# A GpSimd drain placed between the scatters of the last two experts

## The chip, the cores and the metric

The kernel runs on one core of one Trainium2 chip. The metric is the device time of one execution, in microseconds (us), start to end, with the closing barrier of the program inside it. The engines go by the profile's names: PE (TensorE matmul), PEld (TensorE weight load), DVE (VectorE), ACT (ScalarE), POOL (GpSimd) and SP (SyncE). A "q" behind an engine's name (POOLq, SPq) marks instructions of its queue that the profile does not count as busy: waits, branches, drains.

## The reference

The reference is a delta-rule attention followed by a mixture of experts. The attention (4 batches, 8 heads, 768 steps, head size 48) gives 3072 rows of 384 values. Each row goes to one of 8 experts:

```
logits = x @ w_gate;  expert_idx = argmax(logits)          # x: 3072 x 384
disp[e, counts[e]] = x[i]                                   # rows gathered by expert
h = relu(einsum('ecd,edf->ecf', disp, w1))                  # 384 -> 1024
y = einsum('ecf,efd->ecd', h, w2)                           # 1024 -> 384
out[i] = gate_w[i] * y[expert_idx[i], pos[i]]               # scattered back by token
```

## The kernel before

The first half of the program does the attention and, beside it, the routing: which expert each row goes to, and two tables of row numbers, one for gathering (`src_row`) and one for scattering (`dst_row`). The attention's rows are stored in a buffer in HBM (`xbuf`). The second half, from about 280 us on, is the loop `run` over the 8 experts, ordered by load (`NS`: 512 rows for the first down to 364 for the last).

For each expert the loop does five things. GpSimd issues indirect DMAs that fetch the next expert's weights (`fetch`, `weights`, five DMAs per expert, tile `rw`) and gather its rows (`gather`, tile `xg`). ACT and DVE split fetched weights into a high and a low part (`split`, tiles `hw` and `lw`). `first` computes the hidden layer, eight blocks of 128 columns with nine matmuls each (L1171); ACT takes the relu as the high part `hh` (L1173) and DVE the rest as `hl` (L1174). `second` or, for the experts whose row count fills its tiles well, `rows` computes the second product (L1191 or L1235). `scatter` then multiplies 128 rows by their gate on ACT (L1214, tile `ys`) and issues an indirect DMA on GpSimd that writes them to their places in the output (L1215).

The last two experts (`e` = 6 and 7) both go through `rows`, each in three blocks of rows: 128, 128 and 120 or 108. So each issues three scatters, right after one another in GpSimd's queue. Expert 6 prefetches for expert 7; expert 7 has no successor (`nx` is false), so nothing is fetched, gathered or split in it, and GpSimd has only the three scatters left.

GpSimd's queue runs in program order. Before each scatter stands a wait on the landing of the scatter ahead of it, and the scatter itself waits for ACT's `ys`. Behind the last scatter stand a load of the flag `more` with a branch (L1360, L1361: a general path that is not taken here), and then the program's end (L1421), which the framework writes: SP waits for every DMA that is still open, every engine has a drain, and all five engines meet in a barrier that GpSimd closes; GpSimd then clears the semaphores, and a second barrier follows. Over the program GpSimd issues 98 indirect DMAs: 40 for weights, 29 scatters and 29 gathers (25 of `xg` by `src_row`, and 4 of the first expert's rows).

The order in the second half is set by the framework's scheduler; `issue_after(x)` makes the instructions in its block come behind instruction `x` in the schedule. It adds no semaphore.

Of the kernel before, what the change touches and what calls it, by code (L numbers as in the profile page):

```python
# [54 lines left out]
class Attention:  # L55
# [448 lines left out]
    def run(self):  # L504
        with self.tc.manual_schedule(engines={mybir.EngineType.PE, mybir.EngineType.Activation, mybir.EngineType.DVE, mybir.EngineType.Pool, mybir.EngineType.SP}):
            self.run_()

    def run_(self):
# [16 lines left out]
        for i, (q, k0) in enumerate([(0, 0), (1, 0), (2, 0), (3, 0), (4, 0), (5, 0), (0, 1)]):  # L525
            run(self.scores(q, k0, 1 if i < 2 else 2, banks[i % 4]))
            if i < 2:
                self.causal.clear()
            elif i < 6:
                self.heat(8, HEATS[(i + 1) % 4])  # L530
            if i == 1:
                while not self.rooted:
                    spent += self.advance()
            for job in late[i]:
                job()

            while len(self.causal) > 2:
                while spent < EVICT[i - 2] and "Tc" not in self.sg[0]:
                    spent += self.advance()
                self.causal.pop(0)()  # L540
# [6 lines left out]
        for c in range(KC):  # L547
# [28 lines left out]
            if c == 0:  # L576
                self.update(c, 1, self.residual(c, 1))
                self.solves(c, 1)
                self.product_q(c)
                run(self.scores(1, 1))  # L580
# [427 lines left out]
class Experts:  # L1008
# [201 lines left out]
    def scatter(self, e, i, n, yp, ys=None):  # L1210
        nc, rt = self.nc, self.rt
        if ys is None:
            ys = self.pt.tile([128, DM], F32, name="ys", bufs=4)
        nc.scalar.activation(ys[:n], yp[:n], AF.Copy, scale=rt.gt[:n, i, e : e + 1])  # L1214
        nc.gpsimd.indirect_dma_start(  # L1215
            out=self.out[:, :],
            out_offset=bass.IndirectOffsetOnAxis(ap=rt.dst_row[:n, i, e : e + 1], axis=0),
            in_=ys[:n], in_offset=None, bounds_check=N - 1, oob_is_err=False,
        )
# [18 lines left out]
    def run(self):  # L1238
        for _ in self.split0:
            pass  # L1240
        x = self.x
        yT = None
        for e in range(E):
            nx = e + 1 < E
            if nx:
                for _ in self.fetch(e + 1) if e else self.loading:
                    pass
                xg = self.gather(e + 1)
            split = self.split(e + 1) if nx else iter(())
            hs = self.first(e, x, split, 0, 2)  # L1250
            if yT:
                self.last(e - 1, yT, split)
            hs += self.first(e, x, split, 2, 8)
            if nx:
                x = self.split_x(xg, e + 1)
            yT = None
            if e in DIRECT:
                self.rows(e, hs)
            else:
                yT = self.second(e, hs)  # L1260
            for _ in split:
                pass
# [162 lines left out]
```

## Time and profile before

| what | value |
|---|---|
| median of 3 runs | 519.18 us (518.07 to 519.61) |
| profiled execution | 516.17 us |
| its span, first to last instruction | 514.4 us |
| granted TensorE clock, mean | 0.929 of full speed |
| PE busy | 434.4 us (84%) |
| PEld busy | 382.6 us (74%) |
| DVE busy | 302.9 us (59%) |
| ACT busy | 232.9 us (45%) |
| POOL busy | 142.1 us (28%) |

The profiled execution lasted 516.17 us, of which 514.4 us lie between the first and the last instruction; 1.8 us lie around that span. Busy time counts work on an engine's datapath only. Waits, branches and drains are not in it, nor in the chain of waits, whose last entry is the last counted instruction. They are seen when one asks for a source line: the program's end is L1421 and its beginning L1415.

### The profile page before, as it was taken

The page shows a single profiled execution, that of the slowest core. Times are in us where ns is not written, and L with a number is a line of the kernel's source. Part 1 is how long each engine was busy: PE and PEld are TensorE (multiplying, and loading weights), DVE is VectorE, ACT ScalarE, POOL GpSimd, SP SyncE. Part 2 cuts the span into 40 slices and gives each one's busy share as a digit, 9 for nine tenths or more (in the row PEclk, how much of TensorE's full clock was granted, in tenths as well). Part 3 has the DMA queues.
Part 4 walks back from the last instruction along what each step waited for, and adds up shares of the span by engine and source line. Part 5 has one row for each costly group of instructions (what it writes and reads, how often), then busy time and mean ns, then how long its engine had stood idle before and what let it go on. Part 6 is the DMA issues. An engine that isn't in the chain of part 4 may idle for free. (4 is left out here: it accounts for less than half of the span.)

```text
span 514.4 us, 16636 instructions
## 1 busy us (share of the span) xinstructions
PE 434.4 (84%) x7010; PEld 382.6 (74%) x7020; DVE 302.9 (59%) x973; ACT 232.9 (45%) x549; POOL 142.1 (28%) x146
## 2 busy tenths in 40 slices
PE   5673558798997989688879989999999999999990
PEld 3343446676776777566769878899999999999990
DVE  2899899688989983435652565273350817263210
ACT  2115123455766666356522554273562828363210
POOL 8002000100000111456354273434143453520110
PEclk9995577878999999979988999999999999999996
DMA  8882477867866455753162174526145453620000
GB/s 212 189 249 80 114 195 206 246 188 195 208 196 162 99 139 134 197 174 105 34 203 105 55 281 156 169 87 198 72 159 170 152 189 98 204 78 17 29 32 14
DMA packets 51683, 74.45 MB, mean 145 GB/s; under 512 B 28571, under 2 KB 37717, under 8 KB 51602
## 3 DMA queue, kind: packets, MB, share of 16 engines
q1 hardware_dynamic: 39810, 31.78, 23.9%
q0 software_dynamic: 9280, 34.98, 20.0%
q10 hardware_dynamic: 2512, 6.55, 4.5%
q8 instruction: 57, 0.93, 0.8%
q14 instruction: 24, 0.20, 0.1%
HBM read 60.97 MB, written 12.43 MB: 143 GB/s over the span
## 5 line engine op out<-in xcount | busy, mean ns | idle before, releaser
L1174 DVE SCALAR_TENSOR_TENSOR hl<-hp,hh 128x256 fp32r<-128x256 f32 (+7 forms) x64 | 35.5, 555 | 100.2 <-ACT hh L1173 98.9
L1171 PE MATMUL hp<-xh,hw 128*128 128x444 f32 (+6 forms) x168 | 59.1, 354 | 0.0
L1171 PE MATMUL hp<-xl,hw 128*128 128x444 f32 (+6 forms) x168 | 58.1, 346 | 0.0
L1171 PE MATMUL hp<-xh,lw 128*128 128x444 f32 (+6 forms) x168 | 58.1, 346 | 0.0
L415 ACT COPY x<-s 48x384 f32<-48x384 f32 x92 | 43.6, 474 | 30.6 <-PE s L409 20.7
L1133 DVE TENSOR_TENSOR lw<-rw,hw 128x384 fp32r<-128x384 f32 (+1 forms) x100 | 56.4, 609 | 1.8 <-ACT hw L1132 1.8
L1215 POOL DMA_INDIRECT out_dram<-ys,dst_row x27 | 28.6, 1060 | 102.0 <-ACT ys L1214 60.7
L1132 ACT CAST hw<-rw 128x384 fp32r<-128x384 f32 (+1 forms) x103 | 51.6, 556 | 1.6 <-DMA out_dram<-pk,dst_row 1.6
L1273 POOL DMA_INDIRECT rw<-in_w_dram,widx x40 | 40.9, 1021 | 31.3 <-DVE lw L1133 17.7
L1173 ACT ACTIVATE hh<-hp 128x256 fp32r<-128x256 f32 (+7 forms) x64 | 31.4, 491 | 38.2 <-PE hp L1171 35.7
L388 PE MATMUL u<-R,T 64*64 64x48 f32 x736 | 32.5, 228 | 11.2 <-DVE R L378 10.9
L393 ACT ACTIVATE u<-u,mask 128x192 f32<-128x192 f32 x96 | 35.3, 419 | 14.6 <-PE u L388 14.0
L290 DVE TENSOR_TENSOR M<-M,tmp 128x30 f32<-128x30 f32 (+18 forms) x120 | 40.9, 341 | 0.1
L388 PEld LDWEIGHTS u<-R,T 64*64 64x64 f32 x736 | 27.8, 142 | 14.7 <-DVE R L378 13.8
L287 DVE TENSOR_TENSOR tmp<-M,AT 128x96 f32<-128x96 f32 (+33 forms) x124 | 38.5, 342 | 0.1
L378 DVE TENSOR_TENSOR R<-vs,ks 128x192 f32<-128x192 f32 x46 | 16.3, 353 | 31.8 <-PE ks L368 28.2
L1191 PE MATMUL yT<-hh,hw 128*128 128x444 f32 (+3 forms) x96 | 34.1, 359 | 0.0
L1191 PE MATMUL yT<-hh,lw 128*128 128x444 f32 (+3 forms) x96 | 33.8, 355 | 0.0
L1191 PE MATMUL yT<-hl,hw 128*128 128x444 f32 (+3 forms) x96 | 33.0, 354 | 0.0
L1171 PEld LDWEIGHTS hp<-xh,hw 128*128 128x128 f32 x168 | 31.6, 188 | 0.7
L177 PE MATMUL gw<-kb,kd 112*32 112x128 f32 x384 | 18.3, 348 | 16.3 <-DVE P L155 6.7
L1171 PEld LDWEIGHTS hp<-xl,hw 128*128 128x128 f32 x168 | 31.6, 188 | 0.4
(226 smaller groups left out, 982.2 us busy)
## 6 DMA issues: line engine op xcount, KB each, us to landing
kb<-in_kqf_dram SPq DMA_DIRECT2D x24, 192.0 KB
xbuf<-xt SPq DMA_DIRECT2D x24, 192.0 KB
kq<-in_kqf_dram ACTq DMA_DIRECT2D x10, 448.0 KB
kq<-in_kqf_dram SPq DMA_DIRECT2D x10, 448.0 KB
v<-in_vt_dram SPq DMA_DIRECT2D x22, 192.0 KB
k<-in_kt_dram SPq DMA_DIRECT2D x21, 192.0 KB
kd<-in_kqf_dram SPq DMA_DIRECT2D x12, 224.0 KB
mb<-M SPq DMA_DIRECT2D x5, 512.0 KB
```

Of the source, the lines that this page charges most:

```text
L287: nc.vector.tensor_tensor(tv, col.unsqueeze(3).to_broadcast([128, k, m, n]), row.unsqueeze(2).to_broadcast([128, k, m, n]), ALU.mult)
L290: return lambda: nc.vector.tensor_tensor(out, out, tv, alu)
L388: nc.tensor.matmul(us[rows[p], m], T[rows[p], 4 * g + m].rearrange("p a b -> p (a b)"), R[rows[p], m], start=True, stop=True,)
L393: nc.scalar.activation(U[:, 4 * g : 4 * g + 4, o], us, AF.Copy, scale=self.mask[:, 32 + o : 33 + o])
L415: nc.scalar.copy(Xn[rows, ts, :, a].rearrange("p t (h r) d -> p t h r d", h=2), self.S[rows, :, ts].rearrange("p h t r d -> p t h r d"),)
L1132: (nc.scalar.copy if e else self.hi)(hi[p], raw[p])
L1133: (nc.vector.tensor_tensor if e else self.lo)(lo[p], raw[p], hi[p], ALU.subtract)
L1171: nc.tensor.matmul(hp, a, b, start=i == 0, stop=i == len(terms) - 1)
L1173: act = nc.scalar.activation(hh, hp, AF.Relu)
L1174: after = nc.vector.scalar_tensor_tensor(hl, hp, 0.0, hh, ALU.max, ALU.subtract)
L1191: self.nc.tensor.matmul(yT[m], a, b, start=j == 0, stop=j == len(terms) - 1)
L1273: nc.gpsimd.indirect_dma_start(out=raw[:, i * st : i * st + st].rearrange("p k m -> p (k m)"), out_offset=None, in_=tab[:, :], in_offset=b ...
```

## The change

The change keeps a handle on the last scatter that was issued, and in the last expert, behind `first`, it puts one drain instruction on GpSimd that is ordered behind that scatter. At that point of the loop the last scatter is the third one of expert 6.

```diff
@@ scatter
-        nc.gpsimd.indirect_dma_start(
+        self.sent = nc.gpsimd.indirect_dma_start(
             out=self.out[:, :],
...
@@ run
             hs += self.first(e, x, split, 2, 8)
+            if not nx:
+                with self.tc.issue_after(self.sent.ins):
+                    self.nc.gpsimd.drain()
             if nx:
                 x = self.split_x(xg, e + 1)
```

All other instructions of all five engines keep their place, their waits and their addresses; lines behind the loop are numbered 3 higher. GpSimd's queue around the drain is this (drains are left out of such a listing; `ys` numbers tell the scatters apart, the first three are expert 6's, the last three expert 7's):

```order
L1215 DMA out_0_dram<-ys_7237,dst_row_88 3072x384 [waits DMASW4_49,DMASW3_49,Activation_49]
L1215 DMA out_0_dram<-ys_7267,dst_row_88 3072x384 [waits DMASW5_49,DMASW4_49,Activation_49]
L1215 DMA out_0_dram<-ys_7297,dst_row_88 3072x384 [waits DMASW6_49,DMASW5_49,Activation_49]
L1215 DMA out_0_dram<-ys_7440,dst_row_88 3072x384 [waits DMASW7_49,DMASW6_49,Activation_49]
L1215 DMA out_0_dram<-ys_7470,dst_row_88 3072x384 [waits DMASW7_49,Activation_49]
L1215 DMA out_0_dram<-ys_7500,dst_row_88 3072x384 [waits DMASW0_49,Activation_49]
```

The drain stands between the third row and the fourth. It carries no wait on a semaphore and sends none.

## Rows read from the trace of the kernel before

**Rows 1.** The cores: span and granted clock.

```profile
core 0: 514.4 us, clock 0.929
```

**Rows 2.** Busy tenths in 40 slices of the span, PE and POOL.

```profile
PE   5673558798997989688879989999999999999990
...
POOL 8002000100000111456354273434143453520110
```

**Rows 3.** Chain that ended last, its end: start us, us, what.

```profile
494.58 2.60 DMA out_dram<-ys,dst_row
...
498.87 4.72 DMA out_dram<-ys,dst_row
...
503.63 0.58 issue
504.21 0.50 POOLq L1360
504.71 0.75 POOL out_dram L1215
```

**Rows 4.** Timeline of POOL, last scatters: start us, us [idle before <-releaser].

```profile
479.43 1.03 POOL L1215 DMA_INDIRECT out_dram<-ys,dst_row  x1 [2.42 <-issue]
494.58 1.00 POOL L1215 DMA_INDIRECT out_dram<-ys,dst_row  x1 [14.12 <-ACT ys L1214]
498.87 0.98 POOL L1215 DMA_INDIRECT out_dram<-ys,dst_row  x1 [3.29 <-ACT ys L1214]
504.44 1.02 POOL L1215 DMA_INDIRECT out_dram<-ys,dst_row  x1 [4.59 <-DMA out_dram<-ys,dst_row]
```

**Rows 5.** Line L1421, 500 to 510 us: duration ns min/median/max, first and last start.

```profile
L1421 SPq EVENT_SEMAPHORE  x10: 27/28/25422, 482.3 to 508.2; - x10
L1421 SPq DRAIN  x2: 7/10/13, 508.3 to 508.3; - x2
L1421 PEldq DRAIN  x1: 7/7/7, 503.9 to 503.9; - x1
L1421 POOLq DRAIN  x1: 8483/8483/8483, 505.1 to 505.1; - x1
L1421 ACTq DRAIN  x1: 8/8/8, 505.4 to 505.4; - x1
```

**Rows 6.** Line L1421, 510 to 514.4 us, GpSimd's own.

```profile
L1421 POOLq EVENT_SEMAPHORE  x4: 17/17/17, 513.6 to 514.3; - x4
L1421 POOLq DRAIN  x3: 46/113/8483, 505.1 to 514.1; - x3
```

**Rows 7.** Waits of SP's queue, 475 us to the end: us, times, longest.

```profile
SPq L1421 <- PEq L1421: 5.9, 2, 5.4
```

**Rows 8.** Groups of POOL instructions by line: indirect DMAs.

```profile
L1273 POOL DMA_INDIRECT rw<-in_w_dram,widx x40 | 40.9, 1021 | 31.3 <-DVE lw L1133 17.7 <-issue 8.7 <-ACT xT L716 3.4
L1215 POOL DMA_INDIRECT out_dram<-ys,dst_row x27 | 28.6, 1060 | 102.0 <-ACT ys L1214 60.7 <-ACT hh L1173 16.0 <-issue 14.2
L1141 POOL DMA_INDIRECT xg<-xbuf,src_row x25 | 24.0, 959 | 11.5 <-issue 5.8 <-PE tpx L1153 4.3 <-DMA rw<-in_w_dram,widx 0.3
...
L1215 POOL DMA_INDIRECT out_dram<-pk,dst_row x2 | 2.0, 1020 | 2.7 <-ACT hh L1173 2.7
...
L1031 POOL DMA_INDIRECT xg<-xbuf,src x2 | 1.9, 972 | 4.5 <-issue 4.5
L1031 POOL DMA_INDIRECT x<-xbuf,src x2 | 1.9, 960 | 2.5 <-DVE src L898 2.2 <-issue 0.3
```

**Rows 9.** Line L1415, the program's beginning: GpSimd's drain.

```profile
L1415 POOLq DRAIN  x1: 188/188/188, 0.3 to 0.3; - x1
```

**Rows 10.** Timeline of ACT, the gate products of expert 7.

```profile
493.72 0.58 ACT L1214 ACTIVATE ys<-yr,gt 128x384 f32<-128x384 f32 x1 [1.29 <-PE yr L1235]
498.01 0.58 ACT L1214 ACTIVATE ys<-yr,gt 128x384 f32<-128x384 f32 x1 [3.70 <-PE yr L1235]
502.17 0.58 ACT L1214 ACTIVATE ys<-yr,gt 108x384 f32<-108x384 f32 x1 [3.58 <-PE yr L1235]
```

**Rows 11.** Timeline of DVE: beside POOL's scatter, and in its gap.

```profile
479.51 0.54 DVE L1174 SCALAR_TENSOR_TENSOR hl<-hp,hh 128x364 fp32r<-128x364 f32 x1 [9.17 <-ACT hh L1173]
...
486.38 0.54 DVE L1174 SCALAR_TENSOR_TENSOR hl<-hp,hh 128x364 fp32r<-128x364 f32 x1 [1.49 <-ACT hh L1173]
```

**Rows 12.** A stretch: us; PE, PEld, DVE, ACT, POOL busy; clock; DMA share; GB/s.

```profile
480.40:488.40 8.00, 8.00 (x49) 8.00 (x48) 2.15 (x4) 2.38 (x5) 0.06 (x1) 1.00 0.08 21
```

## The prediction

> **What bounds the kernel now.** I read the cores first: one core, a span of 514.4 us [rows 1]. In the forty slices PE is full up to the last one, where it is empty [rows 2]: the expert loop is bound by matmuls, and behind it lies a tail of nearly a slice (12.9 us) in which nearly nothing is counted. The change sits on GpSimd, so the tail matters and PE's loop does not. The chain of waits ends with the last scatter, 504.71 + 0.75 = 505.5 us [rows 3]. That is 8.9 us before the span ends, and no engine is counted busy in them. The reader should take from this that the chain stops at the last counted instruction; what follows has to be asked for by line.
>
> The program's end shows it [rows 5]. SP stands in a wait from 482.3 us for 25.4 us, so until 507.7: that is the landing of the last scatter, whose descriptors were written from 504.44 to 505.46 [rows 4]. SP runs through its remaining waits and is done at 508.3. PE had been done at 503.9 and ACT at 505.4. GpSimd's drain starts at 505.1 and takes 8.483 us, so it ends at 513.6, and there the barrier closes: GpSimd's first event of it is at 513.6, the last at 514.3 [rows 6]. SP waits 5.4 us in that barrier [rows 7]. The row names PE as releaser, but PE's drain was over at 503.9; where the engine named had long been done, it was another, and the only one still at work is GpSimd. So the time from 508.3 to 513.6 belongs to one instruction.
>
> What does that drain do for 5.9 us after the last byte has landed? It does not do it because it is a drain: the one at the program's beginning took 0.188 us [rows 9], and the two behind the long one took 0.046 and 0.113 us [rows 6]. What tells the long one apart is that GpSimd had issued 40 + 27 + 25 + 2 + 2 + 2 = 98 indirect DMAs without a drain between [rows 8]. I read its length as a walk over 98 entries of GpSimd's DMA bookkeeping. If the walk begins when the last descriptors are written, it costs (513.6 - 505.5) / 98 = 83 ns each; if it begins at the landing, (513.6 - 507.7) / 98 = 60 ns. These two are estimates from the rows named.
>
> **The change part by part.** It adds one drain and moves nothing else. There are two places to price.
>
> *The new drain.* It stands behind expert 6's third scatter, written from 479.43 to 480.46, and ahead of expert 7's first, which starts at 494.58 [rows 4]. In that gap GpSimd waits for ACT, whose product ends at 493.72 + 0.58 = 494.30 [rows 10]. Behind the drain are queued the wait and the scatter of expert 7's first block, nothing else; no other engine waits for GpSimd there, since ACT's `ys` buffers are freed by landings. The trace has no drain in mid-program, so I bound it: from below 0.046 us [rows 6], from above the whole 8.483 us [rows 5]. I take the value nearest to the long row: 95 entries, either 480.5 + 95 x 0.083 = 488.4, or, from a landing like SP's at 482.3 [rows 5], 482.3 + 95 x 0.060 = 488.0 us. Between landing and start the third scatter of expert 7 needed 504.44 - (498.87 + 4.72) = 0.85 us of queue work [rows 3, 4], so the drain has to be over by about 493.7 to cost nothing. It has 5.3 us to spare: cost 0. Nor does it hold up DVE, if it behaves like other work of GpSimd's: DVE's `hl` at 479.51 ran beside a scatter in 0.54 us, as did the one at 486.38 beside nothing [rows 11]. Were DVE held for the whole 8.0 us after 480.4, of which it now uses 2.15 [rows 12], PE could lose at most those 8.0 us; I take 0. A gain here has no row: the scatters before and after the gap take 1.03 and 0.98 to 1.02 us [rows 4], the early ones 1.02 [rows 8], so their length does not depend on how much has piled up.
>
> *The last drain.* It now finds 3 entries. By the first price it needs 505.5 + 3 x 0.083 = 505.7, but must still see the landing at 507.7; by the second 507.7 + 3 x 0.060 = 507.9. With 0.046 to 0.188 us for an empty drain [rows 6, 9] it ends between 507.8 and 508.1. What is late next is SP, whose own drain is at 508.3, a few ns long [rows 5]. So the barrier closes at 508.35 instead of 513.6 us, and the 0.8 us behind it [rows 6] stay.
>
> *The sum.* 513.6 - 508.35 = 5.2 us less, nothing added: span 514.4 - 5.2 = 509.2 us, profiled execution 516.17 - 5.2 = 511.0 us. The median of the three runs, 519.18, lies 3.0 us above the profiled execution; the term is a difference within the tail, and I carry it over: 519.18 - 5.2 = 514.0 us.
>
> The rule that speaks against this: the Trainium skill, "PSUM — Partial Sum Buffer", section "Engine vs sequencer instructions", says that a drain waits for its engine to go fully idle, and names no cost that piles up. By it the last drain would wait for the last scatter alone, an earlier drain would take nothing off it, and the time would stay at 519.2 us. "VectorE: DVE Perf Modes", section "The DRAIN you can't avoid", of the same skill has the drains around a kernel at about 12 ns on all five engines, which gives the same 519.2 us. The trace agrees on SP, PE and ACT, 7 to 13 ns, and disagrees on GpSimd, 46 to 8483 ns [rows 5, 6]. Neither rule says where 5.9 us after the landing come from.
>
> **The rivals.**
>
> *The last drain keeps its length.* The 5.9 us behind the landing could hang on the last scatter itself (some closing work of GpSimd's that only the end of the program meets), or the walk could go over the whole table, used or not. Then the new drain is hidden in the gap all the same, and nothing is gained: 519.2 us. For it: the trace has only one drain behind indirect DMAs, so length and count cannot be told apart. Against it: the drains behind the long one, at 0.046 and 0.113 us, walk no table, used or not; and 5.9 us is more than a whole scatter takes from its start to its landing, 2.60 and 4.72 us for expert 7's first two [rows 3]. This is the case that the two pages above would make of it.
>
> *Half of it stays.* The price need not be even: the last three entries may hold most of a fixed part, or the drain's end may have a wait of its own. With half of the 5.2 us gone the time is 516.6 us. For it: one row cannot show linearity. Against it: the short drains leave no more than 0.188 us of fixed part that every drain has.
>
> *The new drain outlasts its gap: slower.* The walk may be dearer in mid-program, with PE and DVE at work, than in the empty tail. Expert 7's second scatter follows the first's landing and its own 0.85 us; the first lands 2.60 us after its start [rows 3], so it may start as late as 498.87 - 3.45 = 495.4 before the second moves, and the drain may end at 494.6 for nothing: 14.1 us from 480.5, or 148 ns per entry. From there each us is passed on through three scatters in series. The 5.2 us gained are gone at an end of 499.8 (203 ns), and slower by 0.3% (1.6 us) begins at 501.4, or 220 ns. At three times the long row's price, 249 ns, it ends at 504.1 and the time is 514.0 + 9.5 = 523.5 us. For it: no row shows a drain beside other work. Against it: if the walk went on only while DVE is idle, 5.85 of 8.0 us [rows 12], the 7.9 us would become 10.8 and end at 491.3, still in time.
>
> **How the numbers follow.** My forecast, 514.0 us, has 0.78; half of it 0.08; no change 0.11; slower 0.03. A difference under 0.3%, 1.6 us, is about what a measurement of this kernel cannot tell from no change. So faster by more than that is 0.78 + 0.08 = 0.86, within it 0.11, slower 0.03. The runs of before spread by 1.5 us, about 0.9 to each side of a middle, and the tail ahead of the drain varies too: expert 7's second scatter took 4.72 us to land, its first 2.60 [rows 3], and the third, whose product was ready at 502.17 + 0.58 = 502.75 [rows 10], started only at 504.44 [rows 4]. So the forecast's own range is 512.4 to 515.6. At the top I reach to the half case, 516.8; the 519.2 and 523.5 us are left out with 0.14, and some 0.05 below.
>
> **What would show it right or wrong.** In the profile after: a GpSimd drain in the run's loop that starts near 479 us and lasts 8 to 9 us, over before 490; expert 7's first scatter still about 0.3 us behind ACT's product; the drain of the program's end about 3 us long instead of 8.5, over with the landing; SP's wait in the barrier at under 0.5 us instead of 5.4; the tail from the last scatter's start to the span's end at 4.7 us instead of 9.9. If both drains are long, the count of entries is not the price. If the new one is short and the last long, closing work of the program's end is. If the new one ends past 494 and expert 7's scatters move, the walk is dearer beside other work.

## The result and the profile after

The change takes the median from 519.14 us (6 runs) to 510.36 us (6 runs, 509.87 to 513.09). The ratio is 0.9882, with a 95% interval of 0.9846 to 0.9918, that is 4.3 to 8.0 us less. The ratio is taken from fast runs alone and is not the quotient of the two medians, which is 0.983 (8.8 us less) and lies outside that interval. The forecast, 5.2 of 519.2 us, is a ratio of 0.990 and lies inside. The profiled execution took 509.87 us, with a span of 508.1 us where before had 514.4 [rows 1].

The new drain, by its own line in the changed kernel (name, count, then duration in ns and start in us, as in [rows 5]):

```profile
L1256 POOLq DRAIN  x1: 9113/9113/9113, 479.4 to 479.4; - x1
```

It ends at 479.4 + 9.1 = 488.5 us. POOL's timeline of the changed kernel answers to [rows 4]:

```profile
479.62 1.03 POOL L1215 DMA_INDIRECT out_dram<-ys,dst_row  x1 [2.42 <-issue]
494.78 1.00 POOL L1215 DMA_INDIRECT out_dram<-ys,dst_row  x1 [14.13 <-ACT ys L1214]
499.06 0.98 POOL L1215 DMA_INDIRECT out_dram<-ys,dst_row  x1 [3.29 <-ACT ys L1214]
503.75 1.02 POOL L1215 DMA_INDIRECT out_dram<-ys,dst_row  x1 [3.70 <-ACT ys L1214]
```

Expert 7's first scatter still waits 14.13 us, and still for ACT: the drain lies inside that wait and adds nothing to it. ACT's product ahead of that scatter, and DVE's `hl` beside the drain, answer to [rows 10] and [rows 11]:

```profile
493.92 0.58 ACT L1214 ACTIVATE ys<-yr,gt 128x384 f32<-128x384 f32 x1 [1.29 <-PE yr L1235]
```
```profile
486.58 0.54 DVE L1174 SCALAR_TENSOR_TENSOR hl<-hp,hh 128x364 fp32r<-128x364 f32 x1 [1.49 <-ACT hh L1173]
```

The scatter starts 494.78 - 494.50 = 0.28 us behind ACT's product, as before, and `hl` takes 0.54 us beside the drain, as it did without one. The program's end (now L1424) answers to [rows 5] and [rows 6]:

```profile
L1424 SPq EVENT_SEMAPHORE  x12: 17/28/24152, 482.5 to 508.0; - x12
L1424 POOLq EVENT_SEMAPHORE  x4: 17/17/17, 507.3 to 508.0; - x4
L1424 POOLq DRAIN  x3: 46/113/2393, 504.4 to 507.8; - x3
L1424 SPq DRAIN  x3: 7/7/13, 507.2 to 507.5; - x3
```

SP's long wait ends at 482.5 + 24.15 = 506.6, the last landing. GpSimd's drain, 8.483 us before, now takes 2.393 and ends at 504.36 + 2.39 = 506.75, so 0.16 us behind that landing. SP is ready for the barrier at 507.3 and is the last; GpSimd's first event of the barrier is there, at 507.3, where it was at 513.6. SP's waits answer to [rows 7]:

```profile
SPq L1424 <- PEq L1424: 0.7, 2, 0.5
```

Both rows hold two waits, one in each barrier. By the time stamps the one in the second barrier is 0.53 us before and after, so the 0.5 that is now the longest is that one, and the wait in the barrier that GpSimd closes went from 5.4 to 0.7 - 0.5 = 0.2 us. Seen from the last scatter's start, the program ends 508.1 - 503.75 = 4.3 us later, where it was 514.4 - 504.44 = 10.0 us.

### The profile page after: what moved, and what is told of

The parts are those of the page before. It is cut to its first block, busy times and chain, and to the rows that moved or that the text cites. A ratio compares the mean times of both kernels' runs of the same rounds, so it can differ in the third digit from the quotient of the medians.

```text
span 508.1 us, 16647 instructions
## 1 busy us (share of the span) xinstructions
PE 439.5 (86%) x7020; PEld 384.9 (76%) x7020; DVE 301.7 (59%) x973; ACT 232.1 (46%) x549; POOL 143.8 (28%) x146
## 5 line engine op out<-in xcount | busy, mean ns | idle before, releaser
L1276 POOL DMA_INDIRECT rw<-in_w_dram,widx x40 | 41.0, 1026 | 30.6 <-DVE lw L1133 17.7
```

Source lines behind the costliest of these rows:

```text
L1276: nc.gpsimd.indirect_dma_start(out=raw[:, i * st : i * st + st].rearrange("p k m -> p (k m)"), out_offset=None, in_=tab[:, :], in_offset=b ...
```

## The experiments

Eleven more kernels were run. Absolute times differ from one set of runs to the next by more than the change is worth (the medians of the kernel before, in the four sets, are 519.14, 511.27, 512.53 and 506.10 us, the last from one run), so a ratio is always to before in the same set, and the lengths are read within the tail. Six of the kernels were timed once, for their lengths alone: the drain at the end took 512.31 us (before in its set 511.27), 8 more DMAs of 2 and of 128 rows 508.27 and 505.55 (512.53), the drain twice 496.31, and the drain in expert 1 and in expert 3 510.36 and 501.53 (506.10). Such single times say nothing of a gain: the kernel with 8 more DMAs of 128 rows has a longer closing drain than before, and its time is 7 us under before's median, as its loop ahead of the tail was faster in that execution (expert 7's first scatter starts at 483.4 us in its trace, and at 494.6 in before's).

Below, k is the number of indirect DMAs that GpSimd issued since its last drain, d the end of the newest one's descriptors, and l its landing.

**A drain on another engine.** The same line on SP:

```diff
-                    self.nc.gpsimd.drain()
+                    self.nc.sync.drain()
```

> The drain of the change is put on SP instead of GpSimd, behind the same scatter; GpSimd has none before the program's end. Theory (a drain of GpSimd takes 82.5 ns for each indirect DMA issued since the last one, counted from the moment the newest one's descriptors are written): GpSimd's closing drain still finds 98, ends 98 x 0.0825 = 8.1 us after the last scatter's descriptors, 5 to 6 us after its landing, and the time is that of before, within 0.3%. Rival (any new instruction at that point, or the changed layout of the code, shifts the tail): the time falls by 3 us or more although the closing drain is as long as before.

The ratio to before is 0.9989 (0.9952 to 1.0026). SP's drain did not stand where it was meant to: nothing ties SP's queue to GpSimd's scatter, and the schedule let it run at 4.1 us. So this shows only that one more drain in the program, and its code, gain nothing. The closing drain (k = 98) in that kernel:

```profile
L1256 SPq DRAIN  x1: 128/128/128, 4.1 to 4.1; - x1
L1424 POOLq DRAIN  x3: 46/112/8477, 502.0 to 511.1; - x3
```

It ends 8.08 us behind d, as before's does (513.54 - 505.46 = 8.08), though its landing came 0.4 us earlier behind d.

**A drain behind the last scatter.** No drain in mid-program; one behind the loop:

```diff
             for _ in split:
                 pass
+        with self.tc.issue_after(self.sent.ins):
+            self.nc.gpsimd.drain()
```

> No drain in the middle; one drain of GpSimd directly behind the last scatter, ahead of the load of the flag. Theory: this drain takes the whole 8.1 us from the last scatter's descriptors, and the program's closing drain, which then finds none, under 0.2 us; the span grows by the flag's load behind the drain, 0.5 to 1 us. Rival (the long time belongs to the end of the program, not to a count of indirect DMAs): the explicit drain ends with the last landing, 2.2 to 3 us after the descriptors, and the closing one still takes 5 us or more.

In that kernel, the last scatter, the explicit drain (L1264) and the program's own (L1423):

```profile
499.66 1.02 POOL L1215 DMA_INDIRECT out_dram<-ys,dst_row  x1 [3.80 <-DMA out_dram<-ys,dst_row]
```
```profile
L1264 POOLq DRAIN  x1: 9343/9343/9343, 499.4 to 499.4; - x1
L1423 POOLq DRAIN  x3: 34/47/107, 509.7 to 510.3; - x3
```

The explicit one ends 8.08 us behind d. The first of the three behind it is at 509.7 and none is longer than 0.107 us. The long time belongs to the first drain behind many indirect DMAs, not to the end of the program. From the last scatter's start to the end it was 510.5 - 499.66 = 10.9 us, 0.9 more than before, as the flag's load now stands behind the drain.

**The drain twice.** The change with its line doubled:

> The change's drain twice in a row. By count, the first takes about 9.1 us and ends 7.8 us after the descriptors of the scatter ahead, the second, with none left, under 0.2 us; the closing one ends 0.16 us after the landing and the tail is the change's. Rival (a drain behind indirect DMAs costs the same each time): the second takes 5 us or more and runs into expert 7's first scatter.

The two drains by their lines, in the columns of [rows 5]:

```profile
L1256 POOLq DRAIN  x1: 9113/9113/9113, 465.6 to 465.6; - x1
L1258 POOLq DRAIN  x1: 47/47/47, 474.8 to 474.8; - x1
```

The second drain takes 0.047 us, so the price of a drain of GpSimd's with nothing to clear is next to nothing.

**Eight more DMAs, small and large.** In the place of the drain stand 8 gathers that nobody reads, of 2 rows in one kernel and of 128 in the other:

```diff
+                more = self.pt.tile([128, NB, DM], F32, name="xg", bufs=1)
                 with self.tc.issue_after(self.sent.ins):
-                    self.nc.gpsimd.drain()
+                    for i in range(8):
+                        self.nc.gpsimd.indirect_dma_start(
+                            out=more[:2, i % 3], out_offset=None, in_=self.rt.xbuf[:, :],
...
```

> No drain in the middle; in its place 8 more gathers on GpSimd of 2 rows each, of data that nobody reads: 106 indirect DMAs before the closing drain. Theory (a fixed price for each DMA, whatever its size): the closing drain ends 106 x 0.0825 = 8.75 us after the last scatter's descriptors, 0.66 us more than before's 8.08. Rival (the price goes by rows, descriptors or bytes): 8 x 2 rows against some 11,000 moved before, under 0.05 us more.

> As the run with 8 more gathers of 2 rows, but of 128 rows each, again of data that nobody reads: 106 indirect DMAs. Theory by count: the closing drain ends 8.75 us after the last scatter's descriptors, as with 2 rows. Rival (price by rows or descriptors): 8 x 128 rows more on some 11,000, about 8.08 x 1.09 = 8.8 us, while the run with 2 rows stays at 8.1.

The last scatter and the closing drain, first with 2 rows:

```profile
495.89 1.02 POOL L1215 DMA_INDIRECT out_dram<-ys,dst_row  x1 [4.25 <-DMA out_dram<-ys,dst_row]
```
```profile
L1429 POOLq DRAIN  x3: 46/113/9142, 496.5 to 506.2; - x3
```

and with 128 rows:

```profile
493.16 1.02 POOL L1215 DMA_INDIRECT out_dram<-ys,dst_row  x1 [4.45 <-DMA out_dram<-ys,dst_row]
```
```profile
L1429 POOLq DRAIN  x3: 46/113/9137, 493.8 to 503.5; - x3
```

With 2 rows the drain runs from 496.50 to 505.64, 8.73 us behind d = 496.90; with 128 rows it is 8.73 as well. That is 0.65 us over before's 8.08 for 8 more DMAs, whatever their size: the price is per DMA, and neither rows nor bytes enter. These kernels also settle what the drain on SP could not: 8 other instructions of GpSimd's in the drain's place do not shorten the closing drain.

**Other counts.** The change with the drain in an earlier expert's loop, here expert 2's; 4, 1 and 3 stand for the 2 in the other kernels:

```diff
-            if not nx:
+            if e == 2:
```

> The drain stands in expert 2's loop instead of the last expert's: 53 indirect DMAs ahead of it, 45 behind. Theory by count from the descriptors: the early drain takes 53 x 0.0825 = 4.4 us from the descriptors of the DMA ahead of it, the closing one ends 45 x 0.0825 = 3.7 us after the last scatter's descriptors, some 1.5 us after its landing; gain over before 8.1 - 3.7 = 4.4 us. Rival (the walk begins at the last landing, at 60 ns each): it ends 45 x 0.060 = 2.7 us after the landing, gain 3.2 us. Rival (a drain clears only what is near it): it stays at 8 us, no gain.

> The drain stands in expert 4's loop: 77 indirect DMAs ahead of it, 21 behind. Theory: it takes 77 x 0.0825 = 6.4 us in a gap of 7.7 us between two scatters; the closing drain could end 21 x 0.0825 = 1.7 us after the last scatter's descriptors, which is before its landing (2.0 to 2.2 us), so it ends about 0.2 us after the landing and SP is the last again. Time: the change's within 0.3%. Rival (every DMA left costs, behind the landing): 18 more than in the change, 18 x 0.06 to 0.083 = 1.1 to 1.5 us more than the change.

The last scatter, the closing drain and SP's barrier wait, with 45 DMAs left:

```profile
499.07 1.02 POOL L1215 DMA_INDIRECT out_dram<-ys,dst_row  x1 [4.39 <-DMA out_dram<-ys,dst_row]
```
```profile
L1424 SPq EVENT_SEMAPHORE  x12: 17/28/25582, 477.1 to 505.3; - x12
L1424 POOLq DRAIN  x3: 46/113/4844, 499.7 to 505.1; - x3
```
```profile
SPq L1424 <- PEq L1424: 1.9, 2, 1.4
```

and with 21 left:

```profile
501.47 1.02 POOL L1215 DMA_INDIRECT out_dram<-ys,dst_row  x1 [4.17 <-DMA out_dram<-ys,dst_row]
```
```profile
L1424 SPq EVENT_SEMAPHORE  x12: 17/28/24658, 479.7 to 506.0; - x12
L1424 POOLq DRAIN  x3: 46/113/3160, 502.1 to 505.8; - x3
```

Both kernels are faster than before, 0.9861 (0.9784 to 0.9937) and 0.9883 (0.9805 to 0.9961), but the lengths fit none of the written cases. With 45 left the drain ends 4.45 us behind d instead of 3.7, which is 1.88 behind the landing instead of 1.5. With 21 left it should have been hidden by the landing and ends 0.90 us behind it; that is 0.74 more than in the change for 18 more DMAs, 41 ns each, half of the price that 98 had shown. A single walk at 82.5 ns is wrong. What fits is two passes of 41 ns per DMA, with the wait for the landing between them: end = max(d + 0.041 k, l) + 0.041 k + 0.04. Two counts that had not been run were forecast from it:

> The drain stands in expert 1's loop: 31 indirect DMAs ahead of it, 67 behind. Two-pass formula, found from the runs so far: a drain ends at max(d + 0.041 k, l) + 0.041 k + 0.04 us, where k is the count of indirect DMAs since the last drain, d the end of the newest one's descriptors and l the last landing. With 67, 2.75 us after d lies behind the landing (1.8 to 2.6 us), so the closing drain ends 2 x 0.041 x 67 + 0.04 = 5.53 us after the last scatter's descriptors. Rival (a price that is not even over the count, the early DMAs being weights for the most part): more than 0.3 us off that.

> The drain stands in expert 3's loop: 62 indirect DMAs ahead of it, 36 behind. Two-pass formula: 36 x 0.041 = 1.48 us after the descriptors lies ahead of the landing, so the closing drain ends 0.041 x 36 + 0.04 = 1.52 us after the landing. Rival (one walk of 82.5 ns per DMA from the descriptors, or until the landing, whichever is later): 2.97 us after the descriptors, 0.4 to 1.1 us after the landing.

The drains of the program's end by line, first in the kernel with 67 left, whose longest is the closing one:

```profile
L1424 POOLq DRAIN  x3: 46/112/5921, 501.8 to 508.3; - x3
```

and in the kernel with 36 left:

```profile
L1424 POOLq DRAIN  x3: 46/113/3730, 495.2 to 499.5; - x3
```

The closing drains end 5.53 us behind d with 67 (forecast 5.53) and 1.51 us behind the landing with 36 (forecast 1.52; the single walk gave 0.4 to 1.1). With 67 the single walk gives 5.53 as well, so of these two it is the one with 36 that decides. The closing drains of eight kernels, and the change's own drain, by the trace's time stamps in us:

| kernel | k | d | l | drain ends | formula |
|---|---|---|---|---|---|
| before | 98 | 505.46 | 507.67 | 513.54 | 513.54 |
| the change, new drain | 95 | 480.64 | 482.44 | 488.48 | 488.47 |
| the change, closing | 3 | 504.76 | 506.59 | 506.75 | 506.75 |
| 8 more DMAs of 2 rows | 106 | 496.90 | 498.84 | 505.64 | 505.63 |
| 8 more DMAs of 128 rows | 106 | 494.18 | 496.49 | 502.92 | 502.91 |
| drain in expert 1 | 67 | 502.21 | 504.68 | 507.74 | 507.74 |
| drain in expert 2 | 45 | 500.09 | 502.66 | 504.54 | 504.55 |
| drain in expert 3 | 36 | 495.58 | 497.40 | 498.91 | 498.92 |
| drain in expert 4 | 21 | 502.49 | 504.36 | 505.26 | 505.26 |

The drains that are not in the table lie within 0.03 us of the formula too: the closing ones of the other kernels, the explicit one at the end, the ones in mid-loop of experts 1 to 4 (k = 31, 53, 62 and 77), and those of the two kernels that follow.

**A drain without a gap.** Between expert 7's first and second scatter, in `rows`, and none behind `first`:

```diff
             self.scatter(e, i, n, yp)
+            if e == E - 1 and i == 0:
+                with self.tc.issue_after(self.sent.ins):
+                    self.nc.gpsimd.drain()
```

> The drain stands between expert 7's first and second scatter, where it has no gap: 96 indirect DMAs ahead of it, 2 behind. Theory: it runs 96 x 0.0825 = 7.9 us from the first scatter's descriptors (about 495.8 to 503.7), holds GpSimd's queue, and the second scatter starts 0.8 us later, at about 504.5 instead of 499.1; the third follows its landing, 4.2 to 5.4 us later than in the change. The closing drain is over with the landing. Time: the change's plus 4.2 to 5.4 us. Rival (a drain does not hold the queue behind it, or works while the queue waits for ACT): both scatters start as in the change and the time is the change's within 0.3%.

The drain by its line, and then POOL's timeline of expert 7's scatters:

```profile
L1239 POOLq DRAIN  x1: 9150/9150/9150, 488.3 to 488.3; - x1
```
```profile
488.55 0.99 POOL L1215 DMA_INDIRECT out_dram<-ys,dst_row  x1 [14.13 <-ACT ys L1214]
498.33 0.98 POOL L1215 DMA_INDIRECT out_dram<-ys,dst_row  x1 [8.78 <-issue]
501.99 1.02 POOL L1215 DMA_INDIRECT out_dram<-ys,dst_row  x1 [2.68 <-DMA out_dram<-ys,dst_row]
```

The drain ends at 497.5, and the second scatter starts 0.87 us later, 9.78 us behind the first where the change has 4.28. The third is 13.44 behind the first, against 8.97: 4.5 us later, inside the 4.2 to 5.4 written. The ratio to before is 1.0019 (0.9972 to 1.0065): a drain in the wrong place gives back what it saves. By the ratios this kernel is 1.4%, some 7 us, slower than the change, with intervals that take in the 4.5 us of the trace. By the trace the tail from expert 7's first scatter on is still 17.7 us against before's 19.8; the times do not show these 2 us.

**A drain in every loop.** The change with `if e > 1:`, six drains:

> A drain in each of the experts 2 to 7: after 53, 62, 77, 89, 92 and 95 indirect DMAs. Theory: they share the 95 between them, 4.4, 0.7, 1.2, 1.0, 0.25 and 0.25 us or the time to the landing of the DMA ahead, each in a gap of GpSimd's except the second, whose gap is 0.3 us, so that gathers behind it start up to 2 us later, hidden by the next expert's lead. Closing drain over with the landing. Time: the change's within 0.3%. Rival (drains delay the weight fetches and PE waits): 1.5 us or more above the change.

The six drains by their line:

```profile
L1256 POOLq DRAIN  x6: 2914/7454/9770, 354.5 to 477.1; - x6
```

The ratio to before is 0.9842 (0.9791 to 0.9893), not told apart from the change's 0.9882; the closing drain ends 0.16 us behind its landing. The lengths went by the landings, which the text had named as the other possibility beside the short times by count: no drain was as short as 0.7 us, and all but the first ended 0.041 k + 0.04 us behind the landing of the DMA ahead. What was not foreseen is how long that is in the loop. The drain with 9 DMAs to clear took 7.2 us, and 5.2 of them lie between its newest descriptors and their landing. So in a busy stretch a drain holds GpSimd's queue for the time of its transfers; the time of the whole kernel does not show that anything came late by it.

## Why the prediction was right

*What bounds the end.* The step that read 5.9 us of the tail as one instruction, and its cause as a count, is shown: the same 8.08 us moves with the first drain behind the DMAs, grows by 0.65 us with 8 DMAs of any size, and is 0.047 us behind another drain.

*The new drain.* Forecast to end at 488.0 to 488.4 us and to cost nothing; it ended at 488.5, and expert 7's first scatter started 494.78 - 479.62 = 15.16 us behind expert 6's third, as before (494.58 - 479.43 = 15.15). That DVE is not held up, which the prediction had put at 0 from scatters alone, holds for the drain: `hl` took 0.54 us beside it. The slower rival needed 148 ns per DMA; the new drain took (488.48 - 480.64) / 95 = 82.5 ns with PE and DVE at work, as the closing one did in the empty tail. The run without a gap shows that the rival's mechanism, passing a late queue on through the scatters in series, is real where the room is missing.

*The last drain.* Forecast to end 0.1 to 0.4 us behind the landing; it ended 0.16 behind it, and SP took over as the last. SP's two waits fell from 5.9 to 0.7 us, so the one in the first barrier by 5.2 us, which is the forecast's term, and the barrier closes right behind SP. The drain took 2.39 us where about 3 was written, and the tail 4.3 us where 4.7 was, as the landing came 0.4 us sooner behind its scatter.

*The sum.* Of the 514.4 - 508.1 = 6.3 us between the two profiles, 5.2 are the term: from SP's last drain to GpSimd's first event of the barrier it was 508.3 to 513.6, and is nothing that shows now. The rest was not forecast: the third scatter started 503.75 - 499.06 = 4.69 us behind the second instead of 504.44 - 498.87 = 5.57, and landed 2.8 us behind its start instead of 3.2, while the loop up to there stood 0.2 us later. The third scatter follows the landing of the second by 0.85 us in both, and that landing took 4.72 us before [rows 3]; in the changed kernel's chain it is

```profile
499.06 3.83 DMA out_dram<-ys,dst_row
```

The gap between these two scatters is 4.8 to 5.6 us in the five kernels without a drain ahead of the last scatter and 4.7 to 5.6 in the seven with one that does not stand between them. So nothing shows that the drain shortens it, and that the changed kernel's profile has the shortest of all is luck. Why the landing varies is not shown; an instruction fetch lies beside the second scatter's packets in both profiles, and was not tried.

*The range.* The median itself, 510.36 us, lies 2.0 us under the written 512.4 to 516.8. By the ratio, 519.18 x 0.9882 = 513.1 us, the result is inside. The width of the range came from three runs of before that spread by 1.5 us; six of them spread by 7.7 (515.51 to 523.24), so it was too narrow for medians of different runs.

*The price.* What was wrong is a step on which this change's time does not hang: 60 or 83 ns per DMA, from one row. It is 41 ns twice, with the landing between. With 95 or 98 DMAs this and a single walk at 82.5 ns cannot be told apart, with 3 neither matters, and only the kernels with 21 to 45 left and the drains in every loop show it. The 60 ns from the landing do not fit: by them the new drain would have ended at 482.44 + 95 x 0.060 = 488.1, and it ended at 488.48.

*The rivals.* No change, which the two rules of the Trainium skill would have given, fell with the closing drain's 2.393 us. One of them, in the Trainium skill's "PSUM — Partial Sum Buffer", section "Engine vs sequencer instructions", has a drain wait until its engine is "fully idle". The traces agree in so far as every drain of GpSimd's with an indirect DMA ahead of it ended at least 0.12 us behind the landing of that DMA; the time per DMA that comes on top is not in that rule. The half that might have stayed did not: a drain with nothing to clear is at 0.047 us.

## What to carry to other kernels

Look at what stands behind the last entry of the chain of waits, and take the lines of the program's end by themselves: a closing drain that outlasts the last landing is time that no busy count shows. Where GpSimd has issued many indirect DMAs, a drain in one of its late waits clears them beside other work; it should come late enough that few remain, since each of those costs behind the last landing, and it needs a gap for its landing and its passes. Put in a queue that has no gap, it gives back what it saves: the kernel with the drain between the last scatters is no faster than before.

## What the hardware showed unexpectedly

GpSimd's drain ended at max(d + 0.041 k, l) + 0.041 k + 0.04 us in all the runs here, from k = 2 to 106, within 0.03 us. This reads as two passes of 41 ns over every indirect DMA since the last drain, with the landing between them; what GpSimd does in a pass, or whether there are two, no trace shows beyond this fit. Whether a DMA moves 2 rows or 128 does not enter, nor whether the other engines work.
